# Strassen's seven block products for the first MLP step of batches 1 to 7 in an FFT-convolution and MLP kernel on one core

## The chip, the cores and the metric

One Trainium2 chip, one of its NeuronCores. The metric is the device time of one execution in microseconds; the median of 3 runs of the kernel before is 2450.35 us (2450.28 to 2451.45).

## The reference

```python
# x (8, 3008, 256); filt_r, filt_i (1505, 256); w_in (256, 2048); w_out (2048, 256)
X = np.fft.rfft(x, axis=1)
y = np.fft.irfft(X * (filt_r + 1j * filt_i)[None], n=3008, axis=1).astype(np.float32)
h = y.reshape(8 * 3008, 256) @ w_in
g = h * (1.0 / (1.0 + np.exp(-1.702 * h)))
return (g @ w_out).astype(np.float32)
```

Each of 8 batches is convolved along its 3008 positions by way of the Fourier transform, and each position then passes a two-layer network (the MLP) with a sigmoid form of GELU between the layers.

## The kernel before, in words

**The transform (FFT).** The length 3008 is 64 times 47, and the transform is two matrix products. `fft(b)` is a generator in 48 steps. Its first stage has 12: for each of six pieces `c`, a load of `x` on SP, a split of the values into a rounded part and a rest (`xh` on ACT, `xl` on POOL, L411 and L412), three matmuls (`mm3`, L275 to L277), and stores of the result to `a_d` in DRAM, issued by ACT (L422). Two empty steps follow, then 16 `forward` and 16 `backward` steps in turn. `forward(i)` takes a slice of `a_d` that POOL's DMA queue has loaded into `zy` (L431), makes four matmuls (L448), adds halves from PSUM (`halves`: ACT copies, L398, DVE adds, L399), multiplies by the filter (`product`: DVE L389 to L391, POOL L392) and writes rounded part and rest back into `zy` (DVE L462, POOL L463). `backward(i)` makes four matmuls on that, adds halves, and stores `b` to DRAM from ACT. Filter slices come by SP into `f_buf` (L181).

**The last stage of the inverse** is `signal(b, t, y)`: for a tile `t` of 512 positions it loads `br` from `b_d`, makes 128-wide matmuls with `t2_sb` (L515), and writes `y`, rounded part and rest (ACT L523, DVE L524). A batch has six such tiles, the last 384 or 512 wide: 64 positions of an even batch are carried to the next.

**The MLP.** Values are kept as a rounded part and a rest (`y[:, 0]`, `y[:, 1]`; `gh`, `gl`), weights too, so each product is three matmuls: rounded by rounded, rounded by rest, rest by rounded. For a tile and a chunk `fc` of 128 of the 2048 hidden units, `first(fc)` makes 2 x 3 matmuls into a PSUM bank `h` (L545; the two are the halves of the 256 inputs), ACT applies the GELU twice (`g` L549, and `gh` rounded, L550), DVE subtracts (`gl`, L551). `second(fc)` makes 6 matmuls (L559) that accumulate in two banks `o` over the 16 chunks. All weights stay in SBUF (`wi_sb`, `wo_sb`). At a tile's end ACT and DVE copy `o` out (L574, L575) and SP stores it.

**The order of the work.** The loop at L611 runs over turns, one chunk of one tile each; `first` runs one chunk ahead of `second`. A batch has 96 turns. In each turn after its chunk the loop lets `fft(b + 1)` go on by so many of its 48 steps that they end 8 turns before the batch does (L633 to L637), and at given chunks lets `signal` of the next tile go on. The order written is not the order run: the framework simulates the program and gives each engine and each DMA queue a fixed order, taking what is ready in the simulation with what was written earlier first. [...] PSUM has eight banks: four shared by all of the FFT and the inverse (`ps_f`), two for `h`, two for `o`. The tag `raw` has seven SBUF buffers, for `x`, `ah`, `al`, `br`, `be`.

Batch 0 has its own transform in front (`first_fft`), in which the weights are loaded, converted from 64 bit and split.

Of the kernel before, what the change touches and what calls it, by code (L numbers as in the profile page):

```python
# [9 lines left out]
F32 = mybir.dt.float32  # L10
F32R = mybir.dt.float32r
# [96 lines left out]
def _places():  # L108

    n1, q = np.arange(N1), np.arange(NH)
    n2 = np.stack([NH - 1 - q, NH + q])
    at = (N2 * n1[None, :, None] + N1 * n2[:, None, :]) % S
    time = np.where(n2[:, None, :] < N2, at, S)
    p, s = np.arange(48)[:, None], np.arange(NS)[None, :]
    k1 = np.where(s == 0, np.where(p < 24, 0, 32), s)
    k2 = np.where(s == 0, p % 24, p)
    freq = (k1 * N2 * pow(N2, -1, N1) + k2 * N1 * pow(N1, -1, N2)) % S
    sign = np.where(freq > S // 2, -1.0, 1.0)  # L120
    freq = np.where(freq > S // 2, S - freq, freq)
    freq = np.where((p < 47) | (s == 0), freq, S // 2 + 1)
    token, odd = [], None
    for b in range(B):
        for t in range(6):
            for i in range(4):
                block = b * S + time[:, :, 4 * t + i]
                if 4 * t + i < NH - 1:
                    token.append(block.ravel())
                elif b % 2 == 0:  # L130
                    odd = block[0]
                else:
                    token += [odd, block[0]]
    return time, freq, np.concatenate(token), sign
# [16 lines left out]
def tile_kernel(  # L151
# [34 lines left out]
    tab = const.tile([P, sum(WIDTHS.values())], F32, name="tab")  # L186
# [7 lines left out]
    t2_sb, sign = table["t2"], table["sign"]  # L194
# [75 lines left out]
    b_of, stores, done_w = {}, [], [0]  # L270
# [8 lines left out]
    banks = [(ps_f, "f"), (ps_o, "o"), (ps_f, "f"), (ps_h, "h")]  # L279
    n_bank = [0]  # L280

    def bank(name):

        pool, tag = banks[n_bank[0] % 4]
        n_bank[0] += 1
        return pool.tile([P, 2, D], F32, tag=tag, name=name)
# [16 lines left out]
    def first_fft():  # L303
# [7 lines left out]
        f_s = [f_buf] + [sb.tile([Q, 4, 2, D], F32, tag="y", name=f"f_y{i}") for i in range(2)]  # L311
# [11 lines left out]
        for c in range(6):  # L323
            load_in(xrs[c], x[0, c])
            if c == 3:
                pin(nc.scalar.dma_start(tab[:, w:], tabs[:, w:]))
        for u in u_buf:
            pin(nc.vector.memset(u[32:64], 0.0))
# [72 lines left out]
    def fft(b):  # L401

        a_d = dram.tile([2, 48, 64, D], F32, tag="a_d", name=f"a_d{b}")
        for c in range(6):
# [3 lines left out]
            for u in range(2):  # L408
# [4 lines left out]
                ps = ps_f.tile([P, 2, D], F32, tag="f", name=f"s1_{b}_{c}_{u}")  # L413
# [26 lines left out]
        def second(i, m, src, name):  # L440

            ps = [ps_f.tile([P, 2, D], F32, tag="f", name=f"{name}_{b}_{i}_{k}") for k in range(2)]
# [52 lines left out]
    def signal(b, t, y):  # L495

        if b:
# [4 lines left out]
            br = [br[:, :, P * m : P * m + P] for m in range(2)]  # L502
        yield
        full = 4 if t < 5 else 3
        for m in range(2):
            if b == 0:
                ps = ps_f.tile([P, 4, P], F32, tag="f", name=f"bt_{t}_{m}")
                for i in range(4):
                    q = 4 * (4 * t + i)
                    nc.tensor.transpose(ps[:, i], b_t[:, m, q : q + 4].rearrange("p c s -> p (c s)"), table["eye"])  # L510
                br = {m: sb.tile([P, 4, P], F32, tag="half", name=f"br_{b}_{t}_{m}", bufs=4)}
                (nc.vector.tensor_copy if m else nc.scalar.copy)(br[m], ps)
            ps = ps_f.tile([P, 512], F32, tag="f", name=f"i1_{b}_{t}_{m}")
            for i in range(full):
                nc.tensor.matmul(ps[:, P * i : P * i + P], br[m][:, i], t2_sb, start=True, stop=True)  # L515
            if full == 3:
                nc.tensor.matmul(ps[:, 384:448], br[m][0:64, 3], t2_sb[0:64, 0:64], start=True, stop=True)
            w = P * full
            to = [(y, 0, w, 0)]
            if full == 3:  # L520
                to.append((carry, 0, 64, 384) if b % 2 == 0 else (y, 448, 64, 384))
            for dst, o, w, q in to:
                nc.scalar.copy(dst[:, 0, m, o : o + w], ps[:, q : q + w])  # L523
                nc.vector.tensor_tensor(dst[:, 1, m, o : o + w], ps[:, q : q + w], dst[:, 0, m, o : o + w].bitcast(F32), ALU.subtract)  # L524
            if full == 3 and b % 2:
                nc.gpsimd.tensor_copy(y[:, :, m, 384:448], carry[:, :, m, :].bitcast(F32))  # L526
            yield

    def mlp(b, t, y, nb, halved=False, sums=(ps_o, "o")):

        w = P * nb
        pos = [sums[0].tile([P, 512], F32, tag=sums[1], name=f"o_{b}_{t}_{m}") for m in range(2)]
# [35 lines left out]
        o = sb.tile([P, 2, 512], F32, tag="out", name=f"out_{b}_{t}")  # L573
        nc.scalar.copy(o[:, 0, :w], pos[0][:, :w])  # L574
        nc.vector.tensor_copy(o[:, 1, :w], pos[1][:, :w])  # L575
        stores.append((out[:, :, done_w[0] : done_w[0] + w], o[:, :, :w]))
        done_w[0] += w
# [14 lines left out]
    carry = const.tile([P, 2, 2, 64], F32R, name="carry")  # L592
    b_t = const.tile([P, 2, 96, NS], F32, name="b_t")
    ys = {}

    def start(b, t):
        ys[b, t] = sb.tile([P, 2, 2, 512], F32R, tag="y", name=f"y_{b}_{t}")
        return signal(b, t, ys[b, t])
# [5 lines left out]
    run(start(0, 0))  # L604
    tiles = [(b, t) for b in range(B) for t in range(6)]
# [3 lines left out]
    turns += [(i, fc) for i in range(2, len(tiles)) for fc in range(NFC)]  # L609
    gens, sigs = {}, {}  # L610
    for n, (i, fc) in enumerate(turns):  # L611
        b, t = tiles[i]
        if n % (6 * NFC) == 0:

            lead = 16 if b == 0 else 0
            done, chunk, chunks = 0, 0, 6 * NFC - lead - 8
            nxt = fft(b + 1) if b + 1 < B else iter(())
        if fc == 0:
            sums = (ps_f, "f") if i == 1 else (ps_o, "o")
            gens[i] = mlp(b, t, ys.pop((b, t)), 4 if t < 5 or b % 2 else 3, i < 2, sums)  # L620
# [12 lines left out]
        if b or n >= lead:  # L633
            chunk += 1
            while chunk <= chunks and done < STEPS * chunk // chunks:
                run(nxt, 1)
                done += 1  # L637
        if fc in ((0, 1, 4) if i == 0 else (8, 9, 12) if i == 1 else (9, 12, 14) if t == 5 else (1, 3, 9)) and i + 1 < len(tiles):
            if i + 1 not in sigs:
                sigs[i + 1] = start(*tiles[i + 1])  # L640
            run(sigs[i + 1], 1)
        if fc == NFC - 1:
            run(gens.pop(i))
            if i + 1 in sigs:
                run(sigs[i + 1])
    store()
# [28 lines left out]
```

## Time and profile before

| | |
|---|---|
| median of 3 runs | 2450.35 us |
| span of the profiled execution, first to last instruction | 2449.0 us; the page gives no other time for this execution |
| instructions | 31732 |
| PE, DVE, ACT, POOL busy | 98%, 62%, 54%, 34% of the span |
| granted TensorE clock, mean | 0.993 |
| DMA | 246.60 MB, 101 GB/s over the span |

A row of a group reads: line, engine, operation, output from inputs, shapes and count; then busy us and mean ns of one; then the engine's idle time before such instructions and what ended it. A row of the timeline has the start in us, the duration, engine, line, operation; in brackets idle time before it. A row of waits has the waiting instruction, what it waited for, total us, times, longest. DMA-issuing instructions of ACT and SP are not counted as busy. The rows of stretches give busy us and count for each engine, then the granted clock, the busy share of the DMA engines and GB/s.

### The profile page before, as it was taken

What the parts mean: (1) busy time and instruction counts of PE and PEld (TensorE: products, weight loads), DVE (VectorE), ACT (ScalarE), POOL (GpSimd) and SP (SyncE); (2) the same over time, 40 slices, a digit from 0 to 9 for tenths busy, and PEclk for the clock granted to TensorE, in tenths of its full rate; (3) what the DMA queues carried; (4) which work ended last, traced back from release to release, by engine and by line L of the source; (5) the groups of instructions that cost most, each with busy time, mean ns of one, the idle gap of its engine ahead of it and who ended that gap; (6) DMA issues with size and microseconds to landing.
All of it is one profiled execution on the core that took longest, in us unless ns stands there. A gap on an engine that the chain in (4) does not pass through costs nothing.

```text
span 2449.0 us, 31732 instructions
## 1 busy us (share of the span) xinstructions
PE 2394.4 (98%) x11082; PEld 1986.1 (81%) x11082; DVE 1523.8 (62%) x2167; ACT 1312.0 (54%) x2441; POOL 836.8 (34%) x714
## 2 busy tenths in 40 slices
PE   8889999999999999999999999999999999999999
PEld 6668788877888888888888888988878888898887
DVE  6876884599447883578636785378843777422322
ACT  5665655555555555556555565555555555444443
POOL 4654552355224441344313442234421444000000
PEclk9899999999999999999999999999999999999999
DMA  9244434544454435434344343444334443200000
GB/s 291 87 120 108 105 100 118 142 120 109 122 137 104 102 76 142 120 95 107 98 135 97 95 116 88 126 112 110 86 103 134 100 106 82 67 16 9 18 9 18
DMA packets 140927, 246.60 MB, mean 101 GB/s; under 512 B 15584, under 2 KB 81248, under 8 KB 140768
## 3 DMA queue, kind: packets, MB, share of 16 engines
q1 hardware_dynamic: 62528, 133.72, 19.4%
q10 hardware_dynamic: 53152, 66.80, 10.2%
q0 software_dynamic: 25088, 44.05, 9.2%
q8 instruction: 88, 1.44, 0.3%
q14 instruction: 71, 0.58, 0.1%
HBM read 150.67 MB, written 93.85 MB: 100 GB/s over the span
## 4 chain that ended last, share of the span: by engine, by line
PE 59%; DMA 2%; ACT 1%; ACTq 0%; issue 0%; DVE 0%; SPq 0%; POOLq 0%
PE o L559 26%; PE h L545 26%; PE i L515 2%; PE s L448 1%; PE i L448 1%; DMA b_d<-b 1%; DMA x<-in_x_dram 1%; DMA br<-b_d 1%; PE s L277 0%; PE s L276 0%; PE s L275 0%; ACTq L422 0%; DMA zy<-a_d 0%; DMA a_d<-al 0%; ACT g L549 0%
## 5 line engine op out<-in xcount | busy, mean ns | idle before, releaser
L545 PE MATMUL h<-y,wi 128*128 128x512 f32 (+1 forms) x4608 | 1172.0, 386 | 1.9 <-ACT y L523 1.0
L551 DVE TENSOR_TENSOR gl<-g,gh 128x512 fp32r<-128x512 f32 (+1 forms) x768 | 636.9, 832 | 750.9 <-ACT gh L550 672.3
L545 PEld LDWEIGHTS h<-y,wi 128*128 128x128 f32 x4608 | 861.8, 188 | 172.6 <-ACT y L523 1.4
L549 ACT ACTIVATE g<-h 128x512 f32<-128x512 f32 (+1 forms) x768 | 452.4, 589 | 908.6 <-PE h L545 767.1
L559 PE MATMUL o<-gh,wo 128*128 128x512 f32 (+1 forms) x3072 | 830.1, 389 | 9.3 <-ACT gh L550 8.5
L559 PEld LDWEIGHTS o<-gh,wo 128*128 128x128 f32 x3072 | 569.5, 188 | 128.5 <-ACT gh L550 14.7
L559 PE MATMUL o<-gl,wo 128*128 128x512 f32 (+1 forms) x1536 | 477.3, 387 | 5.5 <-DVE gl L551 5.4
L550 ACT ACTIVATE gh<-h 128x512 fp32r<-128x512 f32 (+1 forms) x768 | 448.8, 585 | 51.0 <-PE o L559 46.7
L463 POOL TENSOR_TENSOR zy<-c_buf,zy 48x512 fp32r<-48x512 f32 x224 | 334.4, 1493 | 93.2 <-DVE zy L462 83.8
L392 POOL TENSOR_TENSOR c_buf<-c_buf,u_buf 112x512 f32<-112x512 f32 x128 | 198.6, 1552 | 417.5 <-DVE c_buf L391 417.3
L559 PEld LDWEIGHTS o<-gl,wo 128*128 128x128 f32 x1536 | 285.6, 188 | 64.9 <-DVE gl L551 10.0
L412 POOL TENSOR_TENSOR xl<-x,xh 128x512 fp32r<-128x512 f32 x84 | 112.7, 1354 | 405.3 <-ACT xh L411 372.7
L431 POOL DMA_DIRECT2D zy<-a_d x224 | 128.3, 575 | 300.5 <-PE s L448 116.0
L399 DVE TENSOR_TENSOR c_buf<-s,c_buf 48x512 f32<-48x512 f32 x224 | 154.2, 689 | 20.2 <-ACT c_buf L398 14.0
L399 DVE TENSOR_TENSOR b<-i,b 48x512 f32<-48x512 f32 x224 | 154.0, 687 | 8.6 <-ACT b L398 2.5
L398 ACT COPY c_buf<-s 48x512 f32<-48x512 f32 x224 | 130.1, 581 | 19.1 <-PE s L448 7.6
L398 ACT COPY b<-i 48x512 f32<-48x512 f32 x224 | 130.2, 581 | 17.0 <-PE i L448 11.7
L462 DVE CAST zy<-c_buf 48x512 fp32r<-48x512 f32 x224 | 96.1, 429 | 49.9 <-POOL c_buf L392 46.2
L515 PEld LDWEIGHTS i<-tab,br 128*128 128x128 f32 x736 | 99.8, 194 | 22.3 <-issue 9.4
L515 PE MATMUL i<-tab,br 128*128 128x128 f32 x736 | 102.7, 279 | 10.5 <-DMA br<-b_d 7.0
L390 DVE TENSOR_TENSOR u_buf<-c_buf,f_buf 48x512 f32<-48x512 f32 x112 | 91.5, 817 | 3.6
L526 POOL CAST y<-carry 128x128 fp32r<-128x128 f32 x8 | 3.2, 429 | 264.3 <-PE h L545 264.1
(88 smaller groups left out, 1266.7 us busy)
## 6 DMA issues: line engine op xcount, KB each, us to landing
f_buf<-fs SPq DMA_DIRECT2D x224, 192.0 KB, 3.3
zy<-a_d POOLq DMA_DIRECT2D x224, 192.0 KB, 3.6
x<-in_x_dram SPq DMA_DIRECT2D x48, 512.0 KB, 5.5
out_dram<-out SPq DMA_DIRECT2D x44, 512.0 KB, 3.5
a_d<-ah ACTq DMA_DIRECT2D x84, 256.0 KB, 3.5
a_d<-al ACTq DMA_DIRECT2D x84, 256.0 KB, 3.8
b_d<-b ACTq DMA_DIRECT2D x112, 192.0 KB, 2.5
br<-b_d SPq DMA_DIRECT2D x84, 256.0 KB, 4.6
```

The lines of the kernel that those rows point to most:

```text
L392: nc.gpsimd.tensor_tensor(u1, u1, u2, ALU.add)
L398: nc.scalar.copy(dst[h], ps[k][o])
L399: nc.vector.tensor_tensor(dst[h], ps[k][h], dst[h], ALU.add)
L412: nc.gpsimd.tensor_tensor(xl, src, xh.bitcast(F32), ALU.subtract)
L431: nc.gpsimd.dma_start(zy[0][64 * k : 64 * k + 48, i % 2].rearrange("p k s d -> p k (s d)"), src.rearrange("n k s d -> n k (s d)"),)
L463: nc.gpsimd.tensor_tensor(y[o, k], u1[h], y[h, k].bitcast(F32), ALU.subtract)
L515: nc.tensor.matmul(ps[:, P * i : P * i + P], br[m][:, i], t2_sb, start=True, stop=True)
L545: nc.tensor.matmul(ps[:, :w], wi_sb[half][:, wk, kc, c], y[:, yk, kc, :w], start=n == 0, stop=n == 5)
L549: nc.scalar.activation(g[:, :w], ps[:, :w], AF.Gelu_apprx_sigmoid)
L550: nc.scalar.activation(gh[:, :w], ps[:, :w], AF.Gelu_apprx_sigmoid)
L551: nc.vector.tensor_tensor(gl[:, :w], g[:, :w], gh[:, :w].bitcast(F32), ALU.subtract)
L559: nc.tensor.matmul(pos[m][:, :w], wo[:, wk, P * m : P * m + P], gp[gk][:, :w], start=fc == 0 and n == 0, stop=fc == NFC - 1 and n == 2,)
```

## The change

From batch 1 on two tiles of positions and two chunks of hidden units are taken together: a 2 x 2 block product (two halves of the inputs, two chunks, two tiles), done with seven products in place of eight by Strassen's scheme in Winograd's form. It uses sums of weight blocks and sums of `y` blocks.

- Batch 0 keeps the old way. During it `sums_of(c)` makes for each of 8 cycles (pairs of chunks) four weight sums on POOL and DVE, splits them, and writes three weight blocks and the four sums to `w_1` and the second step's weights to `w_2` in DRAM. From batch 1 on these are read back in every cycle by SP (`load_1`, `load_2`, 0.92 and 0.52 MB) into rings of three buffers, which lie where the weights lay.
- `pair_signal` takes the place of `signal`: it leaves `y` of both tiles as whole values in `raw` buffers, splits three of the four blocks and makes four sums `t1` to `t4` with DVE, split by ACT and POOL.
- A cycle has four parts `k`. `pa` collects four products one after the other; after each of the first three ACT copies it out (`e1` to `e3`). `pb` has one product, `pg` two. DVE adds the copies to `pb` and `pg` to give three of the four blocks of `h`; the fourth is `pa` itself. ACT applies the GELU twice to each; the rest `gl` is subtracted by POOL for two blocks, by DVE for two. The second step of the cycle before (`second_of`, 24 matmuls) is written between the products.
- The 48 FFT steps of a batch are spread over 82 ticks of 96 (66 in batch 0) in place of 88 (72). Each batch now ends with a 448-wide tile; nothing is carried over.
- PSUM: four banks `h` for the FFT, the inverse and `pa`, `pb`, `pg`; four banks `o`, for two tiles.

The core of the diff:

```diff
-    ps_f = ctx.enter_context(tc.tile_pool(name="ps_f", bufs=4, space=bass.MemoryType.PSUM))
-    ps_h = ctx.enter_context(tc.tile_pool(name="ps_h", bufs=2, space=bass.MemoryType.PSUM))
-    ps_o = ctx.enter_context(tc.tile_pool(name="ps_o", bufs=2, space=bass.MemoryType.PSUM))
+    ps_h = ctx.enter_context(tc.tile_pool(name="ps_h", bufs=4, space=bass.MemoryType.PSUM))
+    ps_o = ctx.enter_context(tc.tile_pool(name="ps_o", bufs=4, space=bass.MemoryType.PSUM))
...
+    def pair_signal(b, u, ops):
...
+        yb, y22, yt = ops["b"], ops["22"], ops["t"]
+        for k, t in enumerate((2 * u, 2 * u + 1)):
...
+            for m in range(2):
+                ps = ps_h.tile([P, 512], F32, tag="h", name=f"i1_{b}_{t}_{m}")
+                inverse_1(brs[k][:, :, P * m : P * m + P], ps, full)
+                (nc.vector.tensor_copy if m else nc.scalar.copy)(to[:, m, :w], ps[:, :w])
+                yield
+            src, hi, lo = (to, yb[:, 0], yb[:, 1]) if k == 0 else (to[:, 1], y22[:, 0], y22[:, 1])
+            nc.vector.tensor_copy(hi, src)
+            nc.gpsimd.tensor_tensor(lo, src, hi.bitcast(F32), ALU.subtract)
...
+        for k, todo in enumerate((((t1, b12, b11), (t3, b22, b12)), ((t2, b22, t1), (t4, b21, t2)))):
+            for o, p, q in todo:
+                nc.vector.tensor_tensor(o, p, q, ALU.subtract)
+            hi, lo = yt[:, 0, 2 * k : 2 * k + 2], yt[:, 1, 2 * k : 2 * k + 2]
+            nc.scalar.copy(hi, ts[k])
+            nc.gpsimd.tensor_tensor(lo, ts[k], hi.bitcast(F32), ALU.subtract)
...
+    LAST = 14
...
+        pace[:] = [0, 0, 6 * NFC - lead - LAST, fft(b + 1) if b + 1 < B else iter(())]
...
+        if n >= 36 and n % 6 == 0 and (n - 36) // 6 < CYCLES:
+            sums_of((n - 36) // 6)
...
+    def product_of(ps, c, a, y, w, first):
+        wt = ring_1[c % 3]
+        for n, (wk, yk) in enumerate(((0, 0), (0, 1), (1, 0))):
+            nc.tensor.matmul(ps[:, :w], wt[:, wk, a], y[yk][:, :w], start=first and n == 0, stop=n == 2, ...)
+
+    def gelu(src, w, cs, on):
+        gh, gl = of(g_h, "h"), of(g_l, "l")
+        nc.scalar.activation(gh[:, :w], src[:, :w], AF.Gelu_apprx_sigmoid)
+        nc.scalar.activation(cs[:, :w], src[:, :w], AF.Gelu_apprx_sigmoid)
+        on.tensor_tensor(gl[:, :w], cs[:, :w], gh[:, :w].bitcast(F32), ALU.subtract)
...
+        for k in range(4):
+            if k == 0:
+                product_of(pa, c, 0, y11, 512, True)
+                e[1] = temp(f"e1_{name}")
+                nc.scalar.copy(e[1], pa)
+                product_of(pb, c, 1, y21, 512, True)
+                cs = of(c_s, "c")
+                nc.vector.tensor_tensor(cs, pb, e[1], ALU.add)
+                gs[0, 0] = gelu(cs, 512, cs, nc.gpsimd)
+                product_of(pg, c, 5, t3, 512, True)
+            elif k == 1:
+                product_of(pa, c, 4, t2, 512, False)
+                e[2] = temp(f"e2_{name}")
+                nc.scalar.copy(e[2], pa)
+            elif k == 2:
+                product_of(pa, c, 3, t1, w1, False)
+                e[3] = temp(f"e3_{name}")
+                nc.scalar.copy(e[3][:, :w1], pa[:, :w1])
+                cs = of(c_s, "c")
+                nc.vector.tensor_tensor(cs[:, :w1], pg[:, :w1], e[3][:, :w1], ALU.add)
+                gs[1, 1] = gelu(cs, w1, cs, nc.gpsimd)
+            else:
+                product_of(pa, c, 6, y22, w1, False)
+                gs[0, 1] = gelu(pa, w1, of(c_s, "c"), nc.vector)
+            second_of(prev, k)
+            if k == 3:
+                product_of(pg, c, 2, t4, 512, False)
+                cs = of(c_s, "c")
+                nc.vector.tensor_tensor(cs, pg, e[2], ALU.add)
+                gs[1, 0] = gelu(cs, 512, cs, nc.vector)
+            tick()
...
+                at = (3, 9, 11, 13, 15, 17) if u < 2 else (20, 23, 24, 25, 26, 27)
+                if slot == at[0]:
+                    sig = start(nb, nu)
+                if slot in at:
+                    run(sig, 1)
```

`start` begins `pair_signal` for the next pair of tiles; `slot` counts the 32 parts of a pair.

More of the change, by code (lines that the diff above doesn't have):

```diff
@@ L501, in signal @@
                 load_in(br[64 * j : 64 * j + 64], b_of[b][n : n + 4].rearrange("n k d -> k n d"))
-            br = [br[:, :, P * m : P * m + P] for m in range(2)]
+            brs.append(br)
         yield
[L504 to L527, printed above, removed]
@@ L538, in mlp, with finish @@
+        yield
+    def finish(pos, w, at, name):
+        o = sb.tile([P, 2, 512], F32, tag="out", name=name)
+        nc.scalar.copy(o[:, 0, :w], pos[0][:, :w])
+        nc.vector.tensor_copy(o[:, 1, :w], pos[1][:, :w])
+        stores.append((out[:, :, at : at + w], o[:, :, :w]))
+    def mlp(b, t, y, w, halved=False):
+        pos = [ps_o.tile([P, 512], F32, tag="o", name=f"o_{b}_{t}_{m}") for m in range(2)]
         gs = {}
@@ L572, in mlp @@
                 first(HALF)
[L573 to L577, printed above, removed]
+        finish(pos, w, S * b + 512 * t, f"out_{b}_{t}")
     def store():
@@ L607, in tile_kernel, with start, next_batch, tick @@
+    ops_of = {}
+    def start(b, u):
+        i = 3 * (b - 1) + u
+        ops_of[b, u] = operands(i)
+        return pair_signal(b, u, ops_of[b, u])
+    LAST = 14
+    pace = [0, 0, 0, iter(())]
+    def next_batch(b, lead):
+        pace[:] = [0, 0, 6 * NFC - lead - LAST, fft(b + 1) if b + 1 < B else iter(())]
+    def tick():
+        pace[0] += 1
+        while pace[0] <= pace[2] and pace[1] < STEPS * pace[0] // pace[2]:
+            run(pace[3], 1)
+            pace[1] += 1
     halves_of = [range(HALF), range(HALF, NFC)]
@@ L608, in tile_kernel @@
     turns = [(i, fc) for h in halves_of for i in range(2) for fc in h]
-    turns += [(i, fc) for i in range(2, len(tiles)) for fc in range(NFC)]
-    gens, sigs = {}, {}
+    turns += [(i, fc) for i in range(2, 6) for fc in range(NFC)]
+    gens, sigs, lead = {}, {}, 16
+    next_batch(0, lead)
     for n, (i, fc) in enumerate(turns):
[L612 to L617, printed above, removed]
@@ L632, in tile_kernel @@
             nc.gpsimd.memset(zy[0][32:64].bitcast(F32), 0.0)
[L633 to L641, printed above, removed]
+        if n >= 36 and n % 6 == 0 and (n - 36) // 6 < CYCLES:
+            sums_of((n - 36) // 6)
+        if n >= lead:
+            tick()
+        if i < 5:
+            if fc in ((0, 1, 4) if i == 0 else (8, 9, 12) if i == 1 else (1, 3, 9)):
+                if i + 1 not in sigs:
+                    ys[i + 1] = y_tile(i + 1)
+                    sigs[i + 1] = signal(i + 1, ys[i + 1])
+                run(sigs[i + 1], 1)
+        elif fc in (4, 7, 8, 10, 11, 13):
+            if fc == 4:
+                sig = start(1, 0)
+            run(sig, 1)
         if fc == NFC - 1:
@@ L646, in tile_kernel @@
+    for k in range(4):
+        second_of(prev, k)
+    store()
     store()
```

196 lines of the change are left out of this document (163 added, 33 removed).

## The prediction, made before the result was known

> **What bounds the kernel now.** I read the page first: the span, the busy shares and the chain.
>
> ```profile
> span 2449.0 us, 31732 instructions
> PE 2394.4 (98%) x11082; PEld 1986.1 (81%) x11082; DVE 1523.8 (62%) x2167; ACT 1312.0 (54%) x2441; POOL 836.8 (34%) x714
> PE   8889999999999999999999999999999999999999
> PE 59%; DMA 2%; ACT 1%; ACTq 0%; issue 0%; DVE 0%; SPq 0%; POOLq 0%
> ```
>
> PE is busy in nearly every slice and is the only large name in the chain that ended last. A busy PE need not be a full one, so I looked at the chain in order of time in the last batch, where nothing but the MLP runs, and at the waits of PE.
>
> ```profile
> 2250.72 1.36 PE o L559 x6
> 2252.08 1.36 PE h L545 x6
> ```
>
> ```profile
> PE o L559 <- ACT gh L550: 8.5, 13, 2.2
> PE o L559 <- DVE gl L551: 5.4, 9, 1.2
> ```
>
> Six matmuls of 512 columns take 1.36 us, 0.2267 us each, with no hole between first and second step; the largest PE wait of the whole span sums to 8.5 us. So PE's stream is the bound, and a matmul removed is worth 0.2267 us as long as the other engines keep up. How near they are to their own limits is seen by stretches: batch 0, a stretch in which the transform (FFT) of the next batch is in its forward/backward steps, one in which it is in its first stage, and the last batch.
>
> ```profile
> core 0: us, PE busy (x) PEld busy (x) DVE busy (x) ACT busy (x) POOL busy (x), PEclk, DMA share, GB/s
> 200.00:400.00 200.00, 192.11 (x916) 160.88 (x914) 159.77 (x227) 112.80 (x212) 98.12 (x82) 1.00 0.44 105
> 1064.00:1184.00 120.00, 120.00 (x542) 98.38 (x541) 97.53 (x137) 68.37 (x124) 57.90 (x51) 1.00 0.42 100
> 1208.00:1304.00 96.00, 94.81 (x442) 78.88 (x441) 32.81 (x47) 48.26 (x89) 15.82 (x12) 1.00 0.46 131
> 2200.00:2400.00 200.00, 200.00 (x897) 165.87 (x896) 57.33 (x86) 84.92 (x158) 0.53 (x2) 1.00 0.03 11
> ```
>
> The reader is to see that the average (DVE 62%, POOL 34%) hides a stretch, two thirds of each batch, with DVE at 0.81 and POOL at 0.48, beside a full PE. The granted clock is 1.00 there and cannot rise.
>
> **What PE saves.** The rows that price PE and the others:
>
> ```profile
> L545 PE MATMUL h<-y,wi 128*128 128x512 f32 x4224 | 1093.6, 391 | 1.9 <-ACT y L523 1.0 <-ACT gh L550 0.9
> L551 DVE TENSOR_TENSOR gl<-g,gh 128x512 fp32r<-128x512 f32 x704 | 592.9, 845 | 678.1 <-ACT gh L550 600.9 <-PE s L277 36.7 <-PE o L559 32.7
> L550 ACT ACTIVATE gh<-h 128x512 fp32r<-128x512 f32 x704 | 417.8, 594 | 45.4 <-PE o L559 41.9
> L463 POOL TENSOR_TENSOR zy<-c_buf,zy 48x512 fp32r<-48x512 f32 x224 | 334.4, 1493 | 93.2 <-DVE zy L462 83.8
> L392 POOL TENSOR_TENSOR c_buf<-c_buf,u_buf 112x512 f32<-112x512 f32 x128 | 198.6, 1552 | 417.5 <-DVE c_buf L391 417.3
> L399 DVE TENSOR_TENSOR c_buf<-s,c_buf 48x512 f32<-48x512 f32 x224 | 154.2, 689 | 20.2 <-ACT c_buf L398 14.0
> L398 ACT COPY c_buf<-s 48x512 f32<-48x512 f32 x224 | 130.1, 581 | 19.1 <-PE s L448 7.6 <-PE s L446 5.1 <-DVE b L399 0.6
> L431 POOL DMA_DIRECT2D zy<-a_d x224 | 128.3, 575 | 300.5 <-PE s L448 116.0 <-PE i L448 52.9 <-DMA a_d<-ah 37.6
> L412 POOL TENSOR_TENSOR xl<-x,xh 128x512 fp32r<-128x512 f32 x84 | 112.7, 1354 | 405.3 <-ACT xh L411 372.7 <-PE h L545 12.8 <-PE o L559 9.1
> L462 DVE CAST zy<-c_buf 48x512 fp32r<-48x512 f32 x224 | 96.1, 429 | 49.9 <-POOL c_buf L392 46.2
> ```
>
> ```profile
> 1400.80 0.89 PE i L515 x8
> ```
>
> Two tiles by two chunks took 8 block products of 3 matmuls; now 7. A pair of full tiles saves 3 matmuls in each of 8 cycles, 24; the pair with the 448-wide tile saves 9216 columns, 18 matmuls. Per batch 66, in 7 batches 462, times 0.2267: **104.7 us off PE**. The second step, the FFT and batch 0 keep theirs; the widths of the last tiles (384/512 to 448/448) keep the total of columns. Per batch PE had 1128 MLP matmuls (255.7 us), 100 of the FFT (22.7) and 92 of the inverse at 0.89/8 (10.2): 288.6 us, a tick (1/96) 3.01 us. Now 273.7, a tick 2.85, a cycle of four ticks 11.4.
>
> **What it adds, per cycle.** On ACT three copies of a PSUM tile (581 each: 1.74 us); the eight activations stay, six now from SBUF. On DVE three adds from PSUM (689) and two `gl` in place of four: 3.75 against 3.38 us. On POOL two `gl`, nearest row L412 at 1354: 2.7 us. Per pair of tiles the operand sums: DVE 4 subtractions, ACT two 1024-wide casts, POOL 3584 columns of low parts. Per batch that is 42 us of copies on ACT, and on POOL 65 for `gl` and 28 for the low parts. All lies beside PE unless an engine runs out.
>
> POOL and DVE don't run beside each other freely. From the timeline, two pairs of rows, and the undisturbed duration from the last batch:
>
> ```profile
> 1414.25 0.69 DVE L551 TENSOR_TENSOR gl<-g,gh 128x512 fp32r<-128x512 f32 x1
> 1414.49 1.60 POOL L392 TENSOR_TENSOR c_buf<-c_buf,u_buf 112x512 f32<-112x512 f32 x1 [4.94 <-DVE c_buf L391]
> 1426.67 1.28 POOL L392 TENSOR_TENSOR c_buf<-c_buf,u_buf 112x512 f32<-112x512 f32 x1 [4.34 <-DVE c_buf L391]
> 1427.03 1.48 DVE L551 TENSOR_TENSOR gl<-g,gh 128x512 fp32r<-128x512 f32 x1 [0.51 <-ACT gh L550]
> ```
>
> ```profile
> L551 DVE TENSOR_TENSOR gl<-g,gh x72: 691/692/693, 2201.1 to 2398.6; 128x512 fp32r<-128x512 f32 x72
> ```
>
> L392 began while a `gl` ran and ended 1.15 us after it (1416.09 less 1414.94); a `gl` that began under L392 ended 0.56 us after it. Each waited for the other, so I count what each holds: 1.15 us for a POOL operation, 0.55 for a DVE one with two SBUF inputs, 0.43 for the cast L462 (its whole row). [...]
>
> A forward/backward pair of FFT steps holds 3x1.15 + 3x0.55 + 2x0.43 = 5.96 us, plus up to 2x0.575 if the two DMA issues of L431 count (no row decides it): 95 to 114 us per batch. Between the first stage (some 22 ticks) and the batch's end stood 74 ticks of 3.01 us, 223, with one `gl` (0.55) each: a demand of 136 to 155, 0.61 to 0.70; at the steps' peak, one pair each 3.67 ticks (11.0 us), 0.72 to 0.83. After: a cycle holds 2x1.15 + 2x0.55, and an eighth of a pair's sums (8.05 + 4x0.55 + 1.29), 4.84 us or 1.21 per tick. 75 ticks of 2.85, 214 us, must hold 95 to 114 + 91: **0.87 to 0.96**. This is the term that decides. Its price per batch lies between nothing (all of it held) and 195/0.82 - 214 = 24 us (no more than the peak before). I take 0.90, 3 us: near the lower end, since 0.72 to 0.83 stood beside a full PE.
>
> ACT is short in the first stage. It also issues the stores there, and they block it without counting as busy:
>
> ```profile
> L422 ACTq DMA_DIRECT2D a_d<-ah x84: 581/616/1582, 131.4 to 1886.6; - x84
> L422 ACTq DMA_DIRECT2D a_d<-al x84: 582/756/2043, 133.5 to 1888.1; - x84
> ```
>
> The stretch of 22 ticks, 66 us, had ACT busy for 0.50 of it (33 us); 24 issues of some 0.69 (17) and 21 ticks' share of the new copies (1.74/4 each, 9) make 59 of the new 60 us. Bounds 0 to 6 us per batch; I take 3.
>
> The weights: 1.44 MB per cycle from SP.
>
> ```profile
> q1 hardware_dynamic: 62528, 133.72, 19.4%
> x<-in_x_dram SPq DMA_DIRECT2D x48, 512.0 KB, 5.5
> SPq L181 <- DVE c_buf L391: 1025.4, 109, 22.5
> ```
>
> q1 moved 133.72 MB in 0.194 of 2449 us, 281 GB/s, so 1.44 MB is 5.1 us of 11.4: 0.45 on top of 0.42 to 0.46. That is 0.9, under 1, and a chunk has two cycles (22.8 us) to land against 5.5 us for 0.5 MB now. I take 0. The upper bound: behind an `f_buf` load SP has waited up to 22.5 us, which uses the whole lead; one such stall of 5 us per batch is 35.
>
> New waits on PE: the products share `pa`, which ACT must copy before the next accumulates, three times a cycle. Behind it all of PE waits; six second-step matmuls (1.36 us, and 0.23 of the last product's own) cover the 0.39 that a matmul takes to end and a copy of 0.58, with 0.62 to spare. FFT tiles, `pa`, `pb` and `pg` now share four banks where the FFT had four alone. Neither is in the trace; the lower end is nothing, since PE has no such wait to lose, the upper is among the rivals. I take 0 for both, as the covers are longer than the rows.
>
> Batch 0 and the hand-over: a tick pace of 66 in place of 72 for the FFT, and weight sums, where PE already loses 7.9 of 200 us (first stretch above); the first cycle has no second step between its products (about three copies, 3 us), and the first operands end some 10 us after fc 13 of tile 5, which has 5.4 us left. It could also win back those 7.9. Bounds -8 and 30; I take 15, the sum of 3, the 5 by which the operands are late and the 7.9 once more.
>
> **Sum**, against the profiled execution: 2449.0 - 104.7 + 15 + 6 x (3 + 3) = 2395.3. The page gives its span alone; the median of the runs, 2450.35, is 1.35 above it, which I add: 2397 us. The last batch has no FFT and keeps its 15.
>
> **Rivals.**
> - All is hidden: 2449.0 - 104.7 + 1.35, up to 15 for the hand-over: 2346 to 2361. For it: DVE's 0.81 cost PE nothing. Against: 0.87 to 0.96.
> - Slower: DVE and POOL bound the forward stretch. If together they fill 0.82 of it, as at most now, six batches lose 24 us: 2346 + 15 + 144 = 2505. It decides below 195/229 = 0.85, where each of six batches gives back the 15 us. For it: POOL's `gl` queue behind DMA issues that wait (116.0 us on PE alone, in the row of L431). Against: the scheduler has 24 ready matmuls of the second step each cycle. [...]
> - ACT's round trip: 504 trips in 7 batches; at 0.3 us each (half an activation ahead in ACT) 151 us, 2500; from 0.18 us it erases the gain. A bank that comes free late works the same way: 76 FFT tiles in each of six batches, 0.2 us each, 91 us. Against: the 0.62 us to spare, ACT at 0.57.
> - Weights late: 2397 + 35 = 2432.
>
> **How the numbers follow.** Forecast 0.46 (its own range 2365 to 2430), all hidden 0.22, DVE/POOL 0.20, ACT 0.07, weights 0.05. The range 2340 to 2470 leaves out half of DVE/POOL's and ACT's cases above and, with the hand-over's lower end in it, little below. A change under 0.2% (5 us) can't be told from none. Faster: 0.46 + 0.22 + 0.05, less the edges: 0.70; same 0.05; slower 0.25.
>
> **What would show it.** Right: first-step matmuls 462 fewer in 512-wide equivalents at 1.36 us per six; PE still the chain; DVE over 0.85 and POOL over 0.75 in forward stretches, with `gl` and POOL means grown; PE waits for ACT, DVE or POOL of some 6 us per batch. Wrong: PE waits of over 15 us per batch there; a chain through POOL or DVE; PE waiting for the DMA of the weights; or a PE without waits.

## The result, and the profile after

| | before | after |
|---|---|---|
| median, us | 2450.9 (2450.28 to 2452.63, 4 runs) | 2707.24 (2700.36 to 2710.64, 4 runs) |
| span of the profiled execution, us | 2449.0 | 2706.6 |
| granted TensorE clock, mean | 0.993 | 0.967 |

The change makes the kernel slower: the ratio of the times is 1.1046, 95% interval 1.1027 to 1.1065. The prediction was 2397 us, with a range that ended at 2470. Its term for the matmuls was right, and 362 us were lost beside it (2706.6 against 2449.0 - 104.7 = 2344.3 by span).

The page of the changed kernel, the lines that answer to the first fence of the prediction:

```profile
span 2706.6 us, 32274 instructions
PE 2447.3 (90%) x10578; PEld 1910.5 (71%) x10578; DVE 1845.9 (68%) x2435; ACT 1638.6 (61%) x2937; POOL 1478.1 (55%) x1149
...
PE   7898899888998889989899898998889989899999
...
PEclk9899999899999999989999999999999989999999
...
PE 9%; DVE 0%; ACT 0%; issue 0%; DVEq 0%
```

PE has 504 instructions fewer (21 a cycle in place of 24, 168 cycles; some of them are 448 wide), but it is busy for 90% in place of 98%, and the 8s are spread over all batches but the last. No other engine is full over the span, and the chain covers only 9% and names PE: neither line points to a culprit. So I went to stretches: the three pairs of tiles of batch 2, and the first pair of batch 7, which has no transform (FFT) beside it.

```profile
core 0: us, PE busy (x) PEld busy (x) DVE busy (x) ACT busy (x) POOL busy (x), PEclk, DMA share, GB/s
776.00:893.00 117.00, 102.72 (x435) 78.10 (x433) 63.00 (x82) 66.20 (x119) 56.07 (x45) 0.97 0.76 216
893.00:1012.00 119.00, 104.81 (x427) 78.67 (x428) 104.03 (x139) 76.90 (x134) 86.80 (x70) 0.96 0.72 195
1012.00:1106.00 94.00, 89.39 (x410) 73.03 (x409) 64.08 (x87) 61.85 (x114) 51.19 (x38) 1.00 0.61 189
2458.00:2541.00 83.00, 82.85 (x381) 68.81 (x380) 39.60 (x49) 50.18 (x89) 29.91 (x19) 1.00 0.49 158
```

The last row is what the change could do: beside no FFT PE is full, and the last batch takes 243.2 us where it took 263.8. Beside the FFT the first two pairs have PE idle for 14 us each. In the second, DVE is at 0.87 and POOL at 0.73, and laying their instructions over each other shows one or the other at work, or held by the other, for 0.96 of the time (0.90 in the second pair of the kernel before, 816 to 918 us). In the first pair that share is only 0.74. The third pair loses little; the FFT ends a little past its half, and the operands of the next pair are made after that.

PE's largest waits, and then one of them in the timeline:

```profile
PE g L756 <- DVE c_f L829: 70.1, 45, 4.5
PE s L269 <- ACT xh L406: 21.8, 17, 3.2
PE o L778 <- POOL wb L765: 16.1, 9, 4.0
```

```profile
955.51 0.58 ACT L827 COPY e<-a 128x512 f32<-128x512 f32 x1
...
956.99 3.44 DVE L457 CAST zy<-c_buf 48x512 fp32r<-48x512 f32 x2
...
957.34 2.36 POOL L547 TENSOR_TENSOR y_bt<-t,y_bt 128x1024 fp32r<-128x1024 f32 x1
...
958.00 0.39 PE L443 MATMUL s<-zy,de_sb 112*112 112x512 f32 x1
...
960.46 1.64 DVE L544 TENSOR_TENSOR t<-y,t 128x512 f32<-128x512 f32 x1
962.13 0.69 DVE L829 TENSOR_TENSOR c_f<-g,e 128x512 f32<-128x512 f32 x1
...
962.87 1.65 PE L756 MATMUL g<-y_a,wa 128*128 128x512 f32 x3 [4.48 <-DVE c_f L829]
...
969.34 0.85 PE L756 MATMUL a<-y_a,wa 128*128 128x512 f32 x3
```

From top to bottom: ACT has copied `pa` out (`e`, L827) by 956.09, so the add L829 could run. In DVE's order it stands behind FFT work, two casts L457 among it, and a subtraction of the operands (L544). The casts, 0.43 us each in the mean of the kernel before (L462), take 3.44, the first of them 2.98 beside POOL's 1024-wide subtraction (L547) and the end of a `gl` just before it; the add starts 6 us after its copy, and the product `t4` can go into `pg` only when the add has read it. PE waits 4.48 us. Then three matmuls, of a kind that takes 0.85 at 969.34, take 1.65: the granted clock is 0.50 there and 1.00 at 969.34. In the whole trace half clock covers 180.2 us, against 38.7 before.

What the held engines look like in the groups, DVE's `gl` (845 ns before) and its cast (429 ns before):

```profile
L765 DVE TENSOR_TENSOR wb<-pc,wb 128x512 fp32r<-128x512 f32 (+1 forms) x135 | 126.3, 936 | 60.0 <-ACT pc L764 59.2
L457 DVE CAST zy<-c_buf 48x512 fp32r<-48x512 f32 x224 | 144.0, 643 | 26.0 <-POOL c_buf L387 21.6
```

### The profile page after: what moved, and what is told of

It is laid out like the page before. It is cut to its first block, busy times and chain, and to the rows that moved or that the text cites. A ratio compares the mean times of both kernels' runs of the same rounds, so it can differ in the third digit from the quotient of the medians.

```text
span 2706.6 us, 32274 instructions
## 1 busy us (share of the span) xinstructions
PE 2447.3 (90%) x10578; PEld 1910.5 (71%) x10578; DVE 1845.9 (68%) x2435; ACT 1638.6 (61%) x2937; POOL 1478.1 (55%) x1149
## 5 line engine op out<-in xcount | busy, mean ns | idle before, releaser
L778 PE MATMUL o<-wb,wc 128*128 128x512 f32 (+1 forms) x1620 | 443.1, 397 | 31.1 <-POOL wb L765 16.1
L778 PEld LDWEIGHTS o<-wb,wc 128*128 128x128 f32 x1620 | 303.6, 191 | 111.0 <-POOL wb L765 23.5
L778 PE MATMUL o<-ph,wc 128*128 128x512 f32 (+1 forms) x1072 | 296.4, 396 | 5.4 <-ACT ph L763 3.9
L829 DVE TENSOR_TENSOR c_f<-g,e 128x512 f32<-128x512 f32 (+1 forms) x168 | 112.2, 668 | 260.7 <-ACT e L827 235.5
L765 POOL TENSOR_TENSOR wb<-c_f,wb 128x512 fp32r<-128x512 f32 (+1 forms) x135 | 179.2, 1327 | 188.3 <-ACT c_f L764 109.5
L765 POOL TENSOR_TENSOR pl<-c_f,ph 128x512 fp32r<-128x512 f32 (+1 forms) x135 | 181.5, 1345 | 178.9 <-ACT c_f L764 92.9
L778 PEld LDWEIGHTS o<-ph,wc 128*128 128x128 f32 x1072 | 203.8, 192 | 53.3 <-ACT ph L763 11.4
L778 PE MATMUL o<-wc 128*128 128x512 f32 (+1 forms) x804 | 226.1, 398 | 10.5 <-POOL wc L765 6.1
L764 ACT ACTIVATE c_f<-c_f 128x512 f32<-128x512 f32 x336 | 208.2, 623 | 14.7 <-DMA br<-b_d 7.0
L827 ACT COPY e<-a 128x512 f32<-128x512 f32 (+1 forms) x168 | 95.5, 569 | 154.8 <-PE a L756 153.3
L778 PE MATMUL o<-pl,wc 128*128 128x512 f32 (+1 forms) x536 | 170.9, 397 | 19.1 <-POOL pl L765 11.2
L778 PEld LDWEIGHTS o<-wc 128*128 128x128 f32 x804 | 151.8, 192 | 49.4 <-POOL wc L765 9.9
L394 DVE TENSOR_TENSOR c_buf<-s,c_buf 48x512 f32<-48x512 f32 x224 | 154.0, 687 | 34.7 <-ACT c_buf L393 30.1
L394 DVE TENSOR_TENSOR b<-i,b 48x512 f32<-48x512 f32 x224 | 153.9, 687 | 27.2 <-ACT b L393 22.1
L457 DVE CAST zy<-c_buf 48x512 fp32r<-48x512 f32 x224 | 144.0, 643 | 26.0 <-POOL c_buf L387 21.6
```

The source lines that it names most:

```text
L394: nc.vector.tensor_tensor(dst[h], ps[k][h], dst[h], ALU.add)
L457: nc.vector.tensor_copy(y[h, k], u1[h])
L764: nc.scalar.activation(cs[:, :w], src[:, :w], AF.Gelu_apprx_sigmoid)
L765: on.tensor_tensor(gl[:, :w], cs[:, :w], gh[:, :w].bitcast(F32), ALU.subtract)
L778: nc.tensor.matmul(pos[t][m][:, :w], wt[:, f, wk, P * m : P * m + P], gp[gk][:, :w], start=first and n == 0, stop=last and n == 2,)
L829: nc.vector.tensor_tensor(cs[:, :w1], pg[:, :w1], e[3][:, :w1], ALU.add)
```

## The experiments

Runs without an interval are one execution each, beside 2707.24 us of the changed kernel, whose own runs lie within 10.3 us; I call smaller differences none. Several leave out work that the result needs. And each edit gives the program other lists of instructions, since the framework orders it anew: in pool_unread, which changes only what PE reads, at least 330 of DVE's 2435 instructions stand elsewhere in its list. No run tells how much of a difference is that reordering. "Pairs" below are the mean durations of a batch's three pairs of tiles over batches 2 to 6, from one copying-out of the outputs to the next; PE's work alone would take 273.7 us per batch, some 91 each. For what was measured in no_pool_new, no_reload, gl_dve and six_banks the expectations held no case; no_adds and late_signal ended 2 us outside theirs.

| kernel | us | against after | pairs, us | half clock, us |
|---|---|---|---|---|
| before | 2450.9 | -256 | 97, 102, 93 | 39 |
| after | 2707.2 | | 120, 119, 97 | 180 |
| no_pool_new | 2584.1 | -123 | 113, 107, 94 | 107 |
| no_pool_gl | 2621.7 | -86 | 116, 111, 94 | 156 |
| pool_unread | 2679.5 | -28 | 117, 117, 98 | 139 |
| gl_dve | 2703.0 | -4 | 113, 120, 102 | 157 |
| pieces | 2713.5 | +6 | 120, 117, 100 | 167 |
| late_signal | 2662.4 | -45 | 115, 118, 96 | 179 |
| no_copies | 2590.1 | -117 | 115, 109, 94 | 160 |
| no_adds | 2702.1 | -5 | 121, 119, 96 | 240 |
| dummy_copies | 2619.3 | -88 | 115, 113, 94 | 161 |
| no_trip | 2727.1 | +20 | 131, 114, 94 | 179 |
| six_banks | 2685.7 | -22 | 117, 118, 97 | 199 |
| six_no_trip | 2743.2 | +36 | 123, 128, 91 | 250 |
| no_reload | 2672.8 | -34 | 117, 115, 99 | 173 |
| no_new_work | 2462.9 | -244 | 104, 103, 87 | 80 |
| no_new_no_reload | 2413.7 | -294 | 97, 103, 87 | 44 |

**POOL's new work left out (no_pool_new).**

```diff
-        on.tensor_tensor(gl[:, :w], cs[:, :w], gh[:, :w].bitcast(F32), ALU.subtract)
+        if on is nc.vector:
+            on.tensor_tensor(gl[:, :w], cs[:, :w], gh[:, :w].bitcast(F32), ALU.subtract)
...
-            nc.gpsimd.tensor_tensor(lo, ts[k], hi.bitcast(F32), ALU.subtract)
```

(`lo` of `src` goes in the same way; what is no longer computed is set to zero once.)

> The changed kernel without the work that the change gives to POOL: the rests gl of two of the four blocks, and the low parts of the y operands, are set to zero once and not computed. Theory A (POOL and DVE hold each other up, their long POOL instructions keep the DVE adds waiting, and PE with them): PE's holes in batches 1 to 6 go, 62 us per batch come back for the most part, 2370 to 2460 us. Rival B (PE waits for ACT's copies and for DVE's adds by their own latency, whatever POOL does): 2620 to 2710. Rival C (the weights' DMA): 2690 to 2710. Rival D (four PSUM banks for FFT and products, too few SBUF buffers): 2600 to 2700.

2584.14, 123 us less: 20.5 per batch with an FFT, where the prediction took 3. DVE's own `gl`, which started 1.01 us after their inputs were there in the mean, now start 0.49 us after, and the FFT's cast is back at its old duration:

```profile
L457 DVE CAST zy<-c_buf 48x512 fp32r<-48x512 f32 x224 | 95.8, 428 | 14.5 <-POOL c_buf L387 9.7
```

**Copies and adds left out (no_copies), and both (no_new_work).** `e[1]` to `e[3]` and the three adds go; the GELU reads `pb` and `pg` in PSUM.

> The changed kernel without the three ACT copies and the three DVE adds of each cycle: the GELUs read the products' PSUM banks directly, so PE no longer waits for a copy before it accumulates. The seven products, POOL's work and the weights stay. Rival B: nearly all of the loss goes, 2350 to 2450 us. Theory A: DVE loses 2 us of work per cycle and PE the adds that it waited for, but POOL and DVE still hold each other; half of the loss goes, 2480 to 2600. Rivals C and D: 2650 to 2710.

> The changed kernel with both left out: POOL's new work (two rests gl of four, the low parts of the y operands) and the three ACT copies and three DVE adds per cycle. What stays of the change: seven products, the weights' loads, two gl on DVE, the operand sums on DVE and ACT, four PSUM banks shared by FFT and products. Left out alone they gave back 123 and 117 us of 2707. If they are separate causes and all: 2360 to 2400. If something else holds the rest (Theory D, the shared PSUM banks and buffers, the order of the instructions): 2440 to 2500, with PE waits for DVE's reading of FFT banks (L394) and for x in the first stage.

2590.11 and 2462.9. The two parts cost 117 and 123 us, and leaving both out saves 244: they add up. So neither is the whole loss, and neither hides the other; 117 us over the 2346 of the saving alone remain.

**The weights loaded once (no_reload; no_new_no_reload with no_new_work's edits).** `load_1` and `load_2` run only for the first three cycles, whose weights serve all.

> The changed kernel with the weights of the first three cycles loaded once and used in all cycles: 240 MB of loads left out. Theory A: 2680 to 2710 us, no change. Rival C (the DMA engines are too full, loads of x, of the filter or of the weights come late): under 2600. Rivals B and D: 2690 to 2710.

> The changed kernel without POOL's new work and without the copies and adds (2463 together) and with the weights of three cycles loaded once and used for all. The PE stream alone would give 2346 to 2361. Theory C (the weights' DMA delays the transform's own loads and stores, or PE by the weights): the 34 us that they cost with all work in place are there again or more, 2410 to 2435. If the 34 came only from POOL's and DVE's queues being late as well, little is left: 2450 to 2463. What then stays above 2361 is batch 0 (441 against 396 in the changed kernel) and the turn between the transform's two halves.

34 us with all else in place, 49 without the rest. Without the rest it is the first pair of a batch that gains (104 to 97 us), where the FFT's first stage loads `x` and stores `a_d`; with all else in place the first two gain 3 and 4 us, and the third loses 2. DMA engines were busy in the first pair for 0.76 of the time (first row of the stretches above), and are for 0.47 in no_new_no_reload:

```profile
726.00:822.00 96.00, 92.42 (x419) 74.74 (x417) 37.88 (x52) 50.78 (x93) 25.69 (x24) 1.00 0.47 123
```

**The kernel before with one suspect each.** `before_gl_pool` gives POOL every `gl` from batch 1 on; `before_banks` shares four PSUM banks between FFT, inverse and `h`, as the changed kernel does.

```diff
+            on = nc.gpsimd if b else nc.vector
-            nc.vector.tensor_tensor(gl[:, :w], g[:, :w], gh[:, :w].bitcast(F32), ALU.subtract)
+            on.tensor_tensor(gl[:, :w], g[:, :w], gh[:, :w].bitcast(F32), ALU.subtract)
```

> The kernel before with one part of the change's kind alone: from batch 1 on every gl is subtracted by POOL in place of DVE. No Strassen, no copies, no loads of weights, PSUM as before. A gl on POOL holds the DVE/POOL pair for 1.15 us in place of 0.55: in forward stretches 5.96 + 3.67 x 1.15 = 10.2 of 11.0 us, 0.92, and 1.0 with POOL's DMA issues. Theory A: slower by 5 to 25 us per batch in the six batches with an FFT, 2480 to 2600 us. Rivals B, C and D: DVE is relieved, 2445 to 2460.

> The kernel before with one part of the change alone: the PSUM banks, four for FFT, inverse and h in common, four for o, in place of four, two and two. Theory D: batch 0, 45 us longer in the changed kernel (441 against 396) with the same MLP as before, becomes 20 to 40 us longer here too, and each later batch a few us; 2475 to 2530. Against it (sums of weights, tick pace and widths make batch 0 longer): 2449 to 2460.

2506.45 (53.5 more than before's 2452.99 beside it) and 2454.29. With 96 `gl` a batch on POOL the FFT's cast goes from 429 to 949 ns: POOL's work costs PE time without any of Strassen's dependences:

```profile
L462 DVE CAST zy<-c_buf 48x512 fp32r<-48x512 f32 x224 | 212.5, 949 | 91.1 <-POOL c_buf L392 86.4
```

Sharing banks by itself costs nothing that can be measured.

**The operands of the second pair made later (late_signal).**

```diff
-                at = (3, 9, 11, 13, 15, 17) if u < 2 else (20, 23, 24, 25, 26, 27)
+                at = (17, 20, 22, 24, 26, 28) if u == 0 else (3, 9, 11, 13, 15, 17) if u == 1 else (20, 23, 24, 25, 26, 27)
```

> The changed kernel with the operands of the second pair of each batch made late in the first pair (slots 17 to 28 in place of 3 to 17), after most of the FFT's first stage. If the first pair's loss (119 us against 93 for the third pair) comes from both wanting the seven raw and four half buffers and DVE/POOL at once: 2600 to 2660 us. If it comes from elsewhere, or only moves into the forward stretch: 2690 to 2730.

2662.36, 45 less, most of it in the first pair (120 to 115 us): the operands no longer fall into the FFT's first stage.

**How POOL's work acts: in pieces, on DVE, unread, `gl` alone.** `pieces` makes four 256-wide instructions of L547; `gl_dve` gives all four `gl` to DVE; in `pool_unread` PE reads the rounded part where it read POOL's rest; `no_pool_gl` leaves out only POOL's `gl`.

```diff
-                gs[0, 0] = gelu(cs, 512, cs, nc.gpsimd)
+                gs[0, 0] = gelu(cs, 512, cs, nc.vector)
```

(gl_dve, the first of its two lines. What its expectation calls the lock are the holds that the prediction counted from its rows, 1.15 us for a POOL operation and 0.55 for a `gl` on DVE.)

> The changed kernel with POOL's subtraction of the low parts of t1 to t4 (L547, one instruction of 2 x 512 columns, 2.4 us) as four instructions of 256 columns. The same elements; POOL holds DVE for as long in sum, or a little longer, but never for more than about 0.7 us at a time. Theory A in the form 'one long hold makes DVE's queue late': 15 to 40 us shorter, 2670 to 2690, L457's longest falls from 2.98 to under 1.5 us. Theory A in the form 'the sum of the holds counts': no gain or up to 15 us longer, 2705 to 2722.

> The changed kernel with all four gl of a cycle on DVE, none on POOL. By the holds of the traces a cycle's hold falls from 4.84 to 3.64 us, a batch's demand by some 22 us; DVE's own time per cycle grows by two gl of 0.7 to 0.9 us, so that DVE alone would have some 0.87 + 0.13 of the second pair's stretch. Theory A (holds and DVE's own lateness): 2630 to 2690, a gain of a part of the 123 that POOL's new work costs. Rival (DVE's own work is the limit, not the lock): slower than 2707, 2710 to 2760.

> The changed kernel with all of POOL's work kept, but PE reads the rounded part in place of every rest that POOL computes (both gl of POOL's and the low parts of the y operands; the values are not the product's). [...] Leaving the work out altogether gave 2584. Theory A1 (the holds slow DVE and POOL, and through their queues the transform): 2660 to 2715. Rival A2 (PE waits for POOL's own late results): 2584 to 2620.

> The changed kernel without POOL's two gl of a cycle (their rest taken as zero), the low parts of the y operands kept: of POOL's new work some 65 of 93 us per batch by the prediction's prices. If the 123 us of both go with POOL's time or its holds, 2615 to 2630. If the long operand instructions (up to 2.75 us each, 8 pieces per pair of tiles) are what makes DVE late, less of it, 2650 to 2690.

2713.54, 2703.0, 2679.47 and 2621.66. Cutting POOL's instruction up gained nothing, but it did not shorten the hold either: the pieces run one after the other, and the longest cast, 2.73 us, lasted through all four of them; beside the one long instruction it was 2.98. So the length of a hold stays untested:

```profile
616.42 3.59 DVE L457 CAST zy<-c_buf 48x512 fp32r<-48x512 f32 x2
616.77 2.96 POOL L549 TENSOR_TENSOR y_a<-t,y_a 128x256 fp32r<-128x256 f32 x4
```

What PE loses by waiting for POOL's results itself is 28 of the 123 us; the other 95 stay when PE reads none of them. The two `gl` make 86 of the 123, and moved to DVE they cost the same as on POOL (the first pair gains 7 us, the third loses 4). The second pair of batch 2 with all `gl` on DVE:

```profile
894.00:1013.00 119.00, 105.49 (x436) 78.96 (x436) 111.67 (x154) 77.91 (x135) 65.89 (x55) 0.97 0.72 195
```

POOL fell from 0.73 to 0.55, DVE rose from 0.87 to 0.94, and the pair of tiles took its 119 us again. There the two engines act as one store of time that is used up (one or the other is at work or held for 0.98 of this stretch). The share is no limit by itself, though: over batches 2 to 6 the second pair of before_gl_pool has 0.94 and takes 101 us, no longer than before, while the first pair of the changed kernel, with 0.72 in the mean, has lost as much of PE's time as the second. What holds up the first pair is shown in parts only: the work left out, the reload and late_signal give back some of it each.

**How copies and adds act (no_adds, dummy_copies, no_trip, six_banks, six_no_trip).** `no_adds` keeps ACT's copies and drops DVE's adds, so that ACT's GELU reads the banks `pb` and `pg` in their place. `dummy_copies` has neither, but three ACT copies per cycle from SBUF. `no_trip` gives each of `pa`'s products its own PSUM tile; the six-bank kernels free two banks by sending both tiles' second step into the same two.

```diff
-                nc.scalar.copy(e[1], pa)
+                nc.scalar.copy(temp(f"e1_{name}"), y11[0].bitcast(F32))
...
+                pa = ps_h.tile([P, 512], F32, tag="h", name=f"a2_{name}")
-                product_of(pa, c, 4, t2, 512, False)
+                product_of(pa, c, 4, t2, 512, True)
```

(The first edit is dummy_copies', the second no_trip's, each for one of three.)

> The changed kernel with ACT's three copies of a cycle kept and DVE's three adds left out: the GELU reads pb and pg straight from PSUM (so the values are not the product's). Without copies and adds the time was 2590 (-117 against 2707). Theory A (the adds stand on a DVE that is held by POOL, so that the bank pg is read late and product t4 waits): nearly all of the 117 goes, 2595 to 2615, and PE's waits for DVE's L829 (70 us, 45 of them) are gone. Rival B (the trip of product to copy to next product in pa is what costs; the adds only follow): most of the 117 stays, 2670 to 2700, and PE waits for ACT's copies instead.

> The kernel without copies and adds (2590), with three ACT copies per cycle put back that read an operand in SBUF in place of pa and that nobody reads: the work of ACT without the trip from product to copy to next product. Theory B1 (ACT's time and its queue are what the copies cost): 2660 to 2705, as with the copies alone (2702). Theory B2 (the trip costs, because the next product must wait for the copy): 2590 to 2625.

> The changed kernel with each of pa's four products in a bank of its own (so they are not summed): copies and adds stay, but no product waits for the copy of the one before; six PSUM tiles per cycle go through the four shared banks in place of three, each held for a shorter time. Theory B2 (the trip): 2590 to 2650. Theory B1 (ACT's and DVE's time): 2680 to 2720, more if banks come free late.

> The changed kernel with two more PSUM banks for what feeds it: the second step of both tiles goes into the same two banks (so the two tiles' outputs are added up), and pa alternates between the two banks that this frees; pb, pg, the transform and the inverse share four. If tiles that wait for a free bank are what the copies and adds cost (they hold pa and pg for longer): 2600 to 2660. If banks don't matter: 2695 to 2720.

> The same with each of pa's four products in the other of the two banks than the one before (so they are not summed): no product waits for the copy of the one before it, and no bank is taken from the transform for that. Theory B2 with banks (the trip costs, and in the kernel without a trip the lack of banks hid it): 2600 to 2650, and clearly under the kernel with six banks and the trip. If ACT's and DVE's own time is what counts, both stay over 2680.

2702.07: without the adds PE's largest wait of the changed kernel is gone, and the time is the same. Its waits moved to the next result of DVE:

```profile
PE o L778 <- DVE pl L765: 41.3, 16, 3.9
PE o L778 <- DVE wb L765: 39.2, 17, 3.9
PE s L269 <- ACT xh L406: 31.2, 15, 4.1
```

My theory that the adds are what costs, drawn from that wait and the timeline above, fell with this run; that DVE is late did not. One of these waits:

```profile
957.06 0.59 ACT L764 ACTIVATE pc<-g 128x512 f32<-128x512 f32 x1
...
959.19 4.27 DVE L457 CAST zy<-c_buf 48x512 fp32r<-48x512 f32 x2 [1.68 <-POOL c_buf L387]
960.38 2.35 POOL L547 TENSOR_TENSOR y_bt<-t,y_bt 128x1024 fp32r<-128x1024 f32 x1
...
963.49 1.64 DVE L765 TENSOR_TENSOR wc<-pc,wc 128x512 fp32r<-128x512 f32 x1
...
965.19 1.22 PE L778 MATMUL o<-wc 128*128 128x512 f32 x2 [3.91 <-DVE wc L765]
```

The `gl` on `wc` had its input at 957.65, but stands in DVE's list behind two casts that first wait for POOL, with DVE idle for 1.68 us, and then run beside its subtraction; it starts 5.8 us later.

The copies as mere work of ACT cost 29 us (2619.26). The wait of product for copy is not the rest: in the changed kernel PE waited 10.7 us in all for copies, and where a product no longer waits for the copy before it the time rose, by 20 and, with six banks, by 58 over the same with the wait (2743.24 against 2685.73). In no_trip the second and third pairs do get shorter (119 to 114, 97 to 94), but the first takes 131, where PE waits 55 us over the span for the FFT's `xh`:

```profile
PE s L269 <- ACT xh L406: 55.0, 30, 5.4
```

Two more banks are worth 22 us. So of the copies' and adds' 117 us, 29 are ACT's time and some 88 appear as soon as the copies read PE's products, in whatever way PE is freed from them. By exclusion I would have put them down to ACT's own order, a copy that waits for its product and holds up FFT work behind it. The traces do not bear that out. In no_adds ACT stood idle for 137.5 us before its copies, and for less than 1 us of this a product of the forward or backward steps was there to be copied; in the first stage, for at most 40 us an `x` was loaded and not yet split, which may as well have waited for one of the four `half` buffers that the copies now share.

What does differ between dummy_copies and no_adds is how long PE waited for DVE's `gl`: 7 us and 98, though the `gl` were about as late in both (0.93 and 0.98 us behind their inputs in the mean). That points to the order of PE's own list, in which a matmul can stand close behind the `gl` that it reads or far, but no run changed the order alone. So the way in which these 88 us arise stays open.

**Strassen in the last batch alone (last_only).** Batches 0 to 6 run the old way with the old banks (four, two, two), batch 7 the new.

> Batches 0 to 6 as before (PSUM as before, 448-wide last tiles, no carry), the weight sums made in batch 6, and Strassen's products in batch 7 alone, where no FFT runs. In the changed kernel the last batch took 243 us against 264 before. Every theory expects that gain of 15 to 20 us, less some 8 for the first cycle and the weight sums in batch 6: 2434 to 2446 us.

2444.17 us (2439.0 to 2448.88, 12 runs) against 2450.69 of before: ratio 0.9973, interval 0.9963 to 0.9983, so 0.3% faster than the kernel before, small but clear of the spread of these runs. The last batch takes 242.5 us, 21 less than before; some 14 of these are given back: batches 2 to 6 take 296 us each in place of 292.4, and batches 0 and 1 end 5 us earlier. Five of both figures only move: the last tile of batch 7 is 448 wide in place of 512, and batches 2, 4 and 6 have a tile of 448 in place of 384. The stretch in which the last batch mostly lies, to be set beside the same one in the prediction:

```profile
2200.00:2400.00 200.00, 200.00 (x920) 167.52 (x919) 87.52 (x114) 123.29 (x220) 70.37 (x47) 1.00 0.46 153
```

## Why the prediction was wrong

- **PE's saving: right.** 462 matmuls in 512-wide equivalents, 104.7 us. The last batch, with nothing beside it, came 20.6 us shorter: the 15 claimed, and 5.4 for its last tile, now 448 wide in place of 512 (24 matmuls' worth of columns, which batches of even number took over).
- **DVE and POOL, 3 us per batch: the first step that failed.** It measured 20.5 (no_pool_new). The demand of 0.87 to 0.96 was a right warning; the choice of 0.90 as nearly free was not, and the bound of 24 us was the better value. The step compared unlike things: 0.72 to 0.83 was the kernel before at the peak of the FFT's steps, 0.87 to 0.96 the mean of 75 ticks of the changed one, 14 of them without FFT steps. At its peak, one pair of steps in 82/24 = 3.42 ticks or 9.7 us, the same prices give 5.96 to 7.11 for the pair and 4.1 for the rest, 10.1 to 11.2 us: 1.04 to 1.15, more than there is. And the idle ticks at the end cannot take it up, as the lists are fixed. (The 0.96 measured in the second pair is another quantity: it also counts time in which one is held by the other, and work that I had priced at no hold.) The account also left out the adds and halves that DVE makes from PSUM. POOL does not lengthen them (the longest L829 took 0.69 us, the longest L394 0.70, where a cast L457 took up to 2.98), but they keep DVE busy too, which may be why moving `gl` to DVE, which by holds alone should have freed 1.2 us a cycle, freed nothing. No run shows what a cast by itself holds, for which I counted 0.43 us, nor whether POOL's DMA issues hold anything; measured is that the cast took 643 ns in the mean, and 428 without POOL's new work. The rival in which DVE and POOL bound the forward stretch (2505, 24 us per batch) was near in this term.
- **PE to ACT and back, 0, with the trip at 151 us as a rival: wrong in size and in mechanism.** Copies and adds cost 117 us, near the rival's figure, but PE waited only 10.7 us for copies, and no_trip did not help: not by the trip that it priced. The covers I counted, six matmuls of the second step, say what PE has to do; they don't say when ACT and DVE get to their part. The framework gives every engine a fixed list, and PE waited 4.48 us for one add that stood behind other work. 29 of the 117 are ACT's time; how the rest arises stays open.
- **The sum took one of the rivals at a time.** Measured, they came together and added up, 123 + 117. Each had been given a chance of its own, so no case held a time of 2700, and the range ended at 2470.
- **ACT's first stage, 3 us: too low, or another term is missing.** 45 us (7.5 per batch) went when the second pair's operands were made after most of that stage. The sum did not place them there, and they are work of all engines, not of ACT alone.
- **Weights, 0, bound 35: wrong, near the bound.** 34 us, or 49 with the other work gone. Not by late weights, as the bound had it: PE's waits in the changed kernel name no load of them. Without the other work the loss lies in the first pair, where the FFT loads and stores; what it is there was not tried.
- **Hand-over and batch 0, 15: about right.** In no_new_no_reload batches 0 and 1 end at 725.7 us. Before they ended at 718.0, and less 15 that is 703, so 23 are lost, of which about 9 is what each later batch loses there too (287.1 against 292.4 - 15, and 1 for the wider last tiles of these batches).
- **"The granted clock is 1.00 there and cannot rise": it fell.** 180.2 us at half clock cost up to 90, against 19 before: some 71 of the lost 362 us. They belong to the terms above, as each wait made them.

The balance by medians: 2707 less 244 (POOL's work, copies and adds) less 49 (reload) gives 2414, and 2346 would have been the saving with nothing lost. Of the last 68, some 23 are batches 0 and 1, about 9 us are in each of the five batches behind, and 2 in the last. What that rest is was not tried.

## What to carry to other kernels

Before work moves off a full PE onto other engines, add up, at the peak of the stretch where it will run and not as a mean, what each will be busy with, DVE and POOL as one if they hold each other up as here, where a cast beside POOL's new work took 643 ns in place of 428 (the prediction's own prices come to over 1 at the peak), and add the terms up rather than choose among them. A wait named by the profile is where the lateness shows, not what it costs: taking away the largest one moved the waiting to the next instruction and saved 5 us, which is within the spread of the runs. Where one stage has idle engines, make the change there alone: one batch of eight gave the only gain found here, 0.3%.

## What the hardware showed beside

In the changed kernel and in no_adds half clock followed short holes. After the first 100 us of the changed kernel PE stood idle 28 times for 2.0 us or more, and with 27 of these a stretch at half clock began, during the idle time or within 2 us of its end; of 130 idle times of 0.5 to 2.0 us, 2 had one, of 1.87 and 1.95 us. In no_adds it was 34 of 46 from 2.0 us on. The stretches last 3.4 us or a multiple (21 of 35 are 3.4; the one that the end of the trace cuts is shorter). By these figures I estimate that a wait of 2.5 us on PE cost about 4.2: itself and half of the 3.4 behind it.
